# An attention and mixer kernel: tiled products gathered into fewer places of TensorE's order, seeds copied ahead of scalings, the fourth tile one stage later

## The chip, the cores and the metric

The kernel runs on one core of a Trainium2 chip. A core has a matmul engine (TensorE, PE in the profile; its weight loads are the row PEld), a vector engine (VectorE, DVE), a scalar engine (ScalarE, ACT), a general one (GpSimd, POOL) and a sync engine whose queue issues most DMAs (SyncE, SP). They run side by side and wait for each other through semaphores. The metric is the device time of one execution in microseconds (us); less is better.

## The reference

Two blocks, one after the other, all in float32. Linear attention without softmax (8 batches, 8 heads, 576 rows, head size 64), each head's output divided by its root mean square, and then a mixer on (8, 576, 512):

```python
kv = einsum('bhsd,bhse->bhde', k, v)
o = einsum('bhsd,bhde->bhse', q, kv)
x = o / sqrt(mean(o * o, axis=-1) + 1e-6) * g_norm      # heads side by side: (8, 576, 512)
h = maximum(x^T @ w_tok1, 0) @ w_tok2                   # over the 576 rows: 576 -> 256 -> 576
u = x + h^T
out = u + maximum(u @ w_ch1, 0) @ w_ch2                 # over the 512 columns: 512 -> 1536 -> 512
```

## The kernel before, in words

The first pass makes u; the second multiplies u with the channel weights by a two-level scheme of seven products for eight, and takes three quarters of the time. The change is in the first pass alone.

The first pass goes through the batches in four pairs. A pair has nine row tiles of 128 rows x 512 columns: four of each batch (rows 0 to 511) and one of the remaining 64 rows of both. They are made two at a time: attention "tiles" c = 0 to 3 (`attend`, L404, two row tiles each) and the remainder c = 4 (`attend_rem`, L418). Work of three pairs is interleaved by hand: `start` (L1241), `middle` (L1247) and the two lists `steady` (L1253) and then `last` (L1302) are strings of step names that `play` (L1192) issues one after the other; each engine executes its own instructions in that order. While a list does attention of pair p + 1 it does token mixing of pair p. Names of steps, with c or the row tile i as digits:

- `kv00 kv01 kv10 kv11` (L364): k^T v of batch 0 or 1 of the pair, half of the heads each, in 128x64 parts of the array; `e..` (L379) copies the result out on ScalarE; `l..` and `lq`, `lr` (L138, L149, L154) issue the loads of the next k, v, q, remainder of q.
- `a0` to `a4`: q times kv, in 64x64 parts of the array, into two PSUM banks, one for each row half; 64 matmul records each in the profile (`ps_o`), 32 for a4 (`ps_r`).
- `q` (squares, ScalarE, L446), `g` (times g_norm out of PSUM, VectorE, L435), `t` (sums of squares, VectorE, L460), then for a group of tiles `m` (mean, L468), `r` (root, ScalarE, L473), `i` (inverse with one correcting step, VectorE, L477), and the scaling of one row tile by the inverse: `s` on ScalarE as eight instructions (L493), `d` on VectorE (L500), `p` on GpSimd (L504).
- `h00 h01 h10 h11` (L532): w_tok1 products of a batch, accumulated over its four row tiles (`ps_h`); `hr` (L539): the remainder rows, 64 rows of the array, and then four relus on ScalarE (L127).
- `u0` to `u8` (L556): w_tok2 products of a row tile (`ps_u`), 4 records each, u8 in 128x64 parts. For i = 2, 4, 6 `z` (`seed`, L550) copies x into the bank beforehand on ScalarE, and the sum is copied out on ScalarE (L130); for the others VectorE adds x (L124). GpSimd issues the stores.
- `f`, digits, `x`, `b`: `f` loads a block of channel weights on SyncE's queue; a digit takes so many steps of their rounding (ScalarE scales, L163 and L166, VectorE clamps, shifts, adds, L169 to L178); `x` transposes row tiles on VectorE and `b` stores them.
- A name with a minus is a step of the pair whose attention began in the list before.

PSUM has eight banks in three pools (L96): "o" 2 (attention), "kv" 2 (k^T v), "h" 4 (token mixing). A tile that takes a bank waits until those that read its former contents are done. The k and v buffers are four, the raw weight buffers four.

Of the kernel before, what the change touches and what calls it, by code (L numbers as in the profile page):

```python
# [11 lines left out]
F32 = mybir.dt.float32  # L12
# [8 lines left out]
def kernel(  # L21
# [33 lines left out]
    P = 128  # L55
    B, S, DM = k.shape
    D = g_norm.shape[0]
# [7 lines left out]
    HP = H // 2  # L65
# [12 lines left out]
    def pool(name, bufs, side="left", stack=ctx, **kw):  # L78
        return stack.enter_context(tc.tile_pool(name=name, bufs=bufs, side=side,
                                                reuse_waits="tile", **kw))  # L80
# [15 lines left out]
    ps = {n: pool(f"ps_{n}", b, "left", psums, space=bass.MemoryType.PSUM)  # L96
          for n, b in (("o", 2), ("kv", 2), ("h", 4))}
# [34 lines left out]
    def matmul(*a, **kw):  # L132
        keep(nc.tensor.matmul(*a, **kw))  # L133
# [220 lines left out]
    def attention(pair, groups):  # L354
# [47 lines left out]
                           rhs=kvp[side][:, hp], start=True, stop=True)  # L402

        def attend(c):  # L404
            o = [ps["o"].tile([P, 2, HP, D], F32, name="ps_o", tag="o") for _ in range(2)]
            side = c // 2
            for t in range(2):
                for hp in range(HP):
                    for n in range(2):
                        for h in range(2):  # L410
                            r = ds(h * D, D)
                            matmul(o[h][ds(n * HF, HF), t, hp],
                                   lhsT=qT[2 * pair + side][r, hp, ds((2 * (c % 2) + t) * P + n * HF, HF)],
                                   rhs=kvp[side][r, hp, :D], start=True, stop=True)
            for h in range(2):
                bank[c, h] = o[h].rearrange("p t k d -> p (t k) d")

        def attend_rem():  # L418
            o = [ps["o"].tile([P, HP, D], F32, name="ps_r", tag="o") for _ in range(2)]
            for hp in range(HP):  # L420
                for side in range(2):
                    for h in range(2):
                        r = ds(h * D, D)
                        matmul(o[h][ds(side * HF, HF), hp], lhsT=q_rest[2 * pair + side][r, hp],
                               rhs=kvp[side][r, hp, :D], start=True, stop=True)
            for h in range(2):
                bank[4, h] = o[h]
# [86 lines left out]
        for c in range(5):  # L514
            if whole:
                steps |= {f"a{c}{t}": do(attend_tile, c, t) if c < 4 else attend_tile_rem
                          for t in range(parts(c))}
            else:
                steps[f"a{c}"] = do(attend, c) if c < 4 else attend_rem
            for h in range(parts(c)):  # L520
                steps |= {f"{n}{c}{h}": do(f, c, h) for n, f in zip("gqt", (gain, square, total))}
            for t in range(1 if c == 4 else 2):
                steps |= {f"{n}{c}{t}": do(f, c, t) for n, f in zip("spd", (scale, scale_pool, scale_vector))}
# [668 lines left out]
    def play(lines, after={}, **stages):  # L1192

        for name in " ".join(lines).split():
            if name.isdigit():
                for _ in range(int(name)):
                    next(stages["rounding"], lambda: None)()
            elif name[0] == "-":  # L1200
                stages["before"][name[1:]]()
            else:
                next(stages[s][name] for s in ("attention", "mixing", "more")
                     if name in stages.get(s, ()))()
# [28 lines left out]
    for block in tok1[2:] + tok2:  # L1233
# [11 lines left out]
        "a21 q21 g20 g21 t20 t21 m2", "h002 h012 r2 i2 d20", "a30 q30 g30", "a31 q31 s21 g31 t30", "h003 h013 t31 m3",  # L1245
        "a40 q40 r3 i3 d30 s31 g40 t40 m4 r4 w21 i4 s40 lq0 l10 l11 lr0 lr1"]
    middle = [  # L1247
        "kv00 e00 w31 w22 w23 w24", "h10 -lq1 w32 w33 w34", "kv01 e01 w41 w42",
        "h11 w43 w44", "hr l00", "a0 q00 g01 q01 g00 t00 t01", "u0 z2 f0", "u1 l01",
        "a1 q10 g11 q11 g10 t10 t11 m0 r0 lq0", "u2 i0", "kv10 e10 z4 d00", "u3 s01", "kv11 e11",  # L1250
        "u4 z6 f1", "a2 q20 g21 q21 g20 s10", "u5 t20 t21 f2", "a4 q40 g41 q41 g40 lr0 lr1 1", "u6 t40 t41 1 l10",
        "a3 q30 g31 q31 g30 lq1 d11", "u7 t30 t31 m2 r2 1 i2 p20 p21 s30", "u8 1 l11 d31"]
    steady = [[  # L1253
        "kv00 kv01 e00 e01 1 -d40 f3", "h00 1 x00", "h01 1 f4 b00", "a0 q00 g01 q01 g00 l00 1",
        "h10 t00 t01 1 x01", "h11 l01 1 x10 b01", "hr 1 x11 z2 f5 f6", "a1 q10 g11 q11 g10 lq0", "kv10 kv11 e10 e11 t10 t11 m0 r0",
        "u0 i0 1", "u1 1 d00 l10", "u2 s01 z4 1 f7", "a2 q20 g21 q21 g20", "u3 s10 t20 t21",
        "u4 z6 l11", "a4 q40 g41 q41 g40 lr0 lr1 1", "u5 d11 t40 t41 1", "a3 q30 g31 q31 g30 lq1",
        "u6 t30 t31 m2 r2 i2 d20 p21 s30", "u7 1 d31 1", "u8 1 b10 b11"], [
        "kv00 kv01 e00 e01 1 -d40 f8", "h00 1 x20", "h01 1 f9", "a0 q00 g01 q01 g00",
        "h10 t00 t01 1 x21", "h11 1", "hr 1 z2 f10", "a1 q10 g11 q11 g10", "kv10 kv11 e10 e11 t10 t11 m0 r0",  # L1260
        "u0 i0 1", "u1 1 d00 f11", "u2 s01 z4 1", "a2 q20 g21 q21 g20", "u3 s10 t20 t21",
        "u4 z6 1 f12", "a4 q40 g41 q41 g40", "u5 d11 t40 t41 1", "a3 q30 g31 q31 g30",
        "u6 t30 t31 m2 r2 i2 d20 p21 s30", "u7 1 d31 b20 b21", "u8 f13"]]

    attentions = [attention(0, ((0,), (1,), (2,), (3,), (4,)))]
    attentions += [attention(p, ((0, 1), (2, 3, 4))) for p in range(1, B // 2)]

    mixings = [token_mixing(p, (2, 4, 6)) for p in range(B // 2 - 1)]
    mixings.append(token_mixing(B // 2 - 1, range(2, 9), (0, 1)))
# [15 lines left out]
    play(middle, attention=attentions[1], mixing=mixings[0], before=attentions[0],  # L1285
         more=more, rounding=rounding)
    for n in range(1, B // 2 - 1):
        play(steady[n - 1], attention=attentions[n + 1], mixing=mixings[n], before=attentions[n],
             more=more, rounding=rounding)


# [5 lines left out]
    for i in range(2):  # L1297
# [2 lines left out]
    woven = fill[0][:4] + fill[1] + fill[0][4:]  # L1300

    last = [  # L1302
        "h00 2 -d40 2 o0", "h01 2 o1", "h10 2 o3", "h11 2 o2", "hr z2 1 o4", "u0 z3 1 c0", "u1 z4 1 c1 o5", "u2 z5 c2",
        "u3 z6 1 c3 o6", "u4 z7 1", "u5 z8 1", "u6 1 s0", "u7 s1 s2", "u8 s3 s4"]
    parts1 = [f for o in ORDER1 for f in split(1, o)]
    more = {f"c{i}": f for i, f in enumerate(t_sums(lambda n: uT[0][:, SB[n]]))}
# [97 lines left out]
```

## Time and profile before

| | us |
|---|---|
| three runs, median (lowest, highest) | 788.10 (786.69, 788.41) |
| the profiled execution | 787.48 |
| span of its core's instructions | 785.7 |
| first pass, first k-v product to the last product of u | 6.2 to 192.3 |
| `middle` (kv00 to the next kv00) | 37.2 to 74.3 |
| first `steady` list | 74.3 to 117.1 |
| second `steady` list | 117.1 to 160.7 |
| `last` | 160.7 to 192.3 |

| stretch | PE busy | DVE busy | ACT busy | POOL busy | DMA GB/s |
|---|---|---|---|---|---|
| 31 to 74 | 42.34 | 31.05 | 28.64 | 2.38 | 347 |
| 74 to 117 | 42.88 | 36.12 | 25.38 | 7.35 | 358 |
| 117 to 160 | 42.29 | 32.71 | 26.46 | 6.19 | 299 |
| 160 to 192 | 32.00 | 27.73 | 17.50 | 6.71 | 279 |

Each stretch of the second table but the last is 43 us long. Busy time of an engine is the union of its instructions; matmuls are pipelined and their ends are modelled, so starts of matmuls are the surer reading. The granted clock of TensorE is full throughout. In a row of a timeline the first number is the start, the second the length of a merged group, both in us from the span's start; "x64" is a number of records, and a bracket names idle time before the group and what ended it.

### The profile page before, as it was taken

To read this page: it belongs to the slowest core of one execution; us is meant where nothing else is said; L and a number is where in the kernel's file an instruction comes from. 1 tells how busy PE (TensorE), PEld (TensorE's weight loads), DVE (VectorE), ACT (ScalarE), POOL (GpSimd) and SP (SyncE) were. 2 spreads that over 40 slices of the span, in tenths; PEclk is the share of its full clock that TensorE was granted. 3 is DMA by queue.
4 is the path that set the end of the run, shared out by engine and by line. 5 is a ranking of instruction groups with operands and counts; after the bars stand their busy time and mean duration, and the time that the engine had idled before them with its cause. 6 is when DMAs were issued, how large, how long until landed. Compare 5 with 4: busy or idle time off the path is not lost.

```text
span 785.7 us, 14826 instructions
## 1 busy us (share of the span) xinstructions
PE 773.3 (98%) x5816; PEld 651.6 (83%) x5816; DVE 614.8 (78%) x909; ACT 269.5 (34%) x531; POOL 71.3 (9%) x84
## 2 busy tenths in 40 slices
PE   6999999999999999999999999999999999999998
PEld 6655545545888888999988899998889999889998
DVE  2877887795776868988778889776998885787977
ACT  2567463845110233521134242123352113325211
POOL 1001112123410000010100001010000101000111
PEclk9999999999999999999999999999999999999999
DMA  9999999787699795598897579889559989655864
GB/s 294 318 330 374 362 360 325 268 267 285 239 286 343 268 329 161 162 294 215 234 248 225 147 216 277 247 200 291 150 154 280 221 213 236 196 150 157 197 171 91
DMA packets 132613, 192.12 MB, mean 245 GB/s; under 512 B 13632, under 2 KB 92224, under 8 KB 132544
## 3 DMA queue, kind: packets, MB, share of 16 engines
q1 hardware_dynamic: 115984, 167.54, 67.8%
q0 software_dynamic: 14656, 22.02, 13.8%
q10 hardware_dynamic: 1904, 1.61, 0.7%
q8 instruction: 46, 0.75, 0.4%
q14 instruction: 23, 0.19, 0.1%
HBM read 138.31 MB, written 52.82 MB: 243 GB/s over the span
## 4 chain that ended last, share of the span: by engine, by line
PE 92%; ACT 3%; DVE 2%; DMA 2%; issue 0%; SPq 0%; ACTq 0%; DVEq 0%
PE ps_d L133 28%; PE ps_b L133 19%; PE ps_a L133 19%; PE ps_u L133 7%; PE ps_h L133 6%; PE ps_v L133 5%; PE ps_c L133 3%; PE ps_w L133 2%; PE ps_o L133 2%; PE ps_kv L133 2%; DMA raw<-in_moe_w_tok_dram 1%; ACT x L498 1%; DMA raw<-in_moe_w_ch_dram 1%; DVE ms L465 1%; DVE x L444 1%; ACT sq L448 1%
## 5 line engine op out<-in xcount | busy, mean ns | idle before, releaser
L133 PE MATMUL ps_d<-ui,w 128*128 128x256 f32 x504 | 118.7, 379 | 0.0
L130 ACT COPY ps_d<-ps_a 128x768 f32<-128x768 f32 (+1 forms) x56 | 32.0, 571 | 215.3 <-PE ps_a L133 215.3
L133 PEld LDWEIGHTS ps_d<-ui,w 128*128 128x128 f32 x504 | 95.1, 190 | 12.8 <-DVE v L124 0.2
L124 DVE TENSOR_TENSOR v<-v,v 128x1536 f32<-128x1536 f32 (+2 forms) x70 | 103.5, 1483 | 0.3
L133 PE MATMUL ps_b<-w,sv 128*128 128x128 f32 x672 | 84.6, 276 | 0.0
L133 PE MATMUL ps_a<-w,v 128*128 128x128 f32 x672 | 84.2, 275 | 0.0
L133 PEld LDWEIGHTS ps_a<-w,v 128*128 128x128 f32 x672 | 79.8, 192 | 0.2
L133 PEld LDWEIGHTS ps_b<-w,sv 128*128 128x128 f32 x672 | 79.5, 192 | 0.2
L133 PE MATMUL ps_u<-h,w_tok 128*128 128x512 f32 (+1 forms) x160 | 67.2, 606 | 0.8 <-ACT ps_u L130 0.7
L133 PE MATMUL ps_h<-x,w_tok 128*128 128x512 f32 (+1 forms) x160 | 65.6, 604 | 0.6 <-DVE x L502 0.4
L133 PE MATMUL ps_d<-w,v 128*128 128x128 f32 x528 | 66.2, 275 | 0.0
L133 PEld LDWEIGHTS ps_d<-w,v 128*128 128x128 f32 x528 | 62.7, 192 | 0.3
L127 ACT ACTIVATE v<-v 128x768 f32<-128x768 f32 (+1 forms) x54 | 42.6, 822 | 55.1 <-DVE v L124 55.1
L133 PE MATMUL ps_d<-w,sv 128*128 128x128 f32 x480 | 60.1, 275 | 0.0
L133 PEld LDWEIGHTS ps_d<-w,sv 128*128 128x128 f32 x480 | 57.1, 192 | 0.2
L133 PEld LDWEIGHTS ps_h<-x,w_tok 128*128 128x128 f32 (+1 forms) x160 | 26.0, 189 | 32.8 <-issue 27.6
L133 PEld LDWEIGHTS ps_u<-h,w_tok 128*128 128x128 f32 (+1 forms) x160 | 24.8, 179 | 31.5 <-issue 25.9
L1121 POOL DMA_DIRECT2D out_dram<-us x11 | 14.2, 1292 | 381.2 <-ACT us L130 268.9
L133 PE MATMUL ps_a<-uT,w 128*128 128x256 f32 x192 | 46.7, 379 | 0.0
L133 PE MATMUL ps_b<-ui,w 128*128 128x256 f32 x168 | 40.8, 379 | 0.0
L133 PEld LDWEIGHTS ps_a<-uT,w 128*128 128x128 f32 x192 | 36.3, 190 | 4.8
L444 DVE TENSOR_TENSOR x<-ps_o,g_sb 128x512 f32<-128x512 f32 x32 | 21.4, 687 | 23.7 <-PE ps_o L133 15.6
(145 smaller groups left out, 1213.0 us busy)
## 6 DMA issues: line engine op xcount, KB each, us to landing
w<-parts SPq DMA_DIRECT2D x168, 384.0 KB, 4.0
w<-parts SPq DMA_DIRECT2D x56, 192.0 KB, 3.0
uT<-blocks SPq DMA_DIRECT2D x36, 256.0 KB, 5.7
k_in<-in_k_dram SPq DMA_DIRECT2D x16, 512.0 KB, 9.0
qT<-in_q_dram SPq DMA_DIRECT2D x8, 1024.0 KB, 9.5
out_dram<-x POOLq DMA_DIRECT2D x16, 512.0 KB, 6.5
v_in<-in_v_dram SPq DMA_DIRECT2D x14, 512.0 KB, 9.1
raw<-in_moe_w_ch_dram SPq DMA_DIRECT2D x8, 768.0 KB, 10.5
```

Of the source, the lines that this page charges most:

```text
L124: keep(engine.tensor_tensor(out=o, in0=a, in1=b, op=op))
L127: keep(nc.scalar.activation(o, a, AF.Relu))
L130: keep(nc.scalar.copy(o, a))
L133: keep(nc.tensor.matmul(*a, **kw))
L444: keep(nc.vector.tensor_mul(x, bank[c, h], g_sb.to_broadcast([P, number(c), D])))
L448: keep(nc.scalar.activation(sq[c, h], bank[c, h], AF.Square))
L465: keep(nc.vector.tensor_reduce(stats_of(c)[0][:, h], sq[c, h], axis=AX.X, op=ALU.add))
L498: keep(nc.scalar.activation(x[:, k, h], x[:, k, h], AF.Copy, scale=inv[:, k, h]))
L1121: keep(nc.gpsimd.dma_start(to.rearrange("t p e -> p t e"), a, accum_op=ALU.add))
```

## The change

- In `middle` and both `steady` lists the places of the tiled products move: h11 follows h10 directly in `middle`; u0, u1 and u2 follow each other; kv10 and kv11 stand directly behind a1 in `middle` too; a4 stands directly behind a2; a3, with everything that belongs to it (q, g, t, s30, d31 and the load lq1), goes to the beginning of the next list, behind kv00, kv01 and the former pair's u8. In the second `steady` list a3 of the last pair stands between u7 and u8, and its scalings at the beginning of `last`.
- a0 and a4 take their banks from the pool "kv" in place of "o".
- In the `steady` lists the seeds z4 and z6 are issued ahead of the eight scalings s01 and s10.
- Tiles are grouped for their statistics as (0, 1), (2, 4), (3) in place of (0, 1), (2, 3, 4).
- The rounding steps, weight loads, transposes and block stores are placed anew along the lists; SyncE's queue gets the loads in another order (lq1, 1 MB, behind f3 and f8; l01 ahead of f0; f7 behind l11). In `last` one rounding step more is left to do.

```diff
         def attend(c):
-            o = [ps["o"].tile([P, 2, HP, D], F32, name="ps_o", tag="o") for _ in range(2)]
+            n = "o" if c else "kv"
+            o = [ps[n].tile([P, 2, HP, D], F32, name="ps_o", tag=n) for _ in range(2)]
...
         def attend_rem():
-            o = [ps["o"].tile([P, HP, D], F32, name="ps_r", tag="o") for _ in range(2)]
+            o = [ps["kv"].tile([P, HP, D], F32, name="ps_r", tag="kv") for _ in range(2)]
...
     middle = [
-        "kv00 e00 w31 w22 w23 w24", "h10 -lq1 w32 w33 w34", "kv01 e01 w41 w42",
-        "h11 w43 w44", "hr l00", "a0 q00 g01 q01 g00 t00 t01", "u0 z2 f0", "u1 l01",
-        "a1 q10 g11 q11 g10 t10 t11 m0 r0 lq0", "u2 i0", "kv10 e10 z4 d00", "u3 s01", "kv11 e11",
-        "u4 z6 f1", "a2 q20 g21 q21 g20 s10", "u5 t20 t21 f2", "a4 q40 g41 q41 g40 lr0 lr1 1", "u6 t40 t41 1 l10",
-        "a3 q30 g31 q31 g30 lq1 d11", "u7 t30 t31 m2 r2 1 i2 p20 p21 s30", "u8 1 l11 d31"]
+        "kv00 e00 w31 w22 w23 w24", "h10 -lq1 w32 w33 w34", "h11 w41 w42 w43 w44", "kv01 e01", "hr l00 z2",
+        "a0 q00 g01 q01 g00 t00 t01", "u0 l01 f0", "u1 z4", "u2", "a1 q10 g11 q11 g10",
+        "kv10 kv11 e10 e11 t10 t11 m0 r0 lq0", "u3 z6 i0 d00 s01 d11 f1", "u4 l10", "a2 q20 g21 q21 g20",
+        "a4 q40 t20 g41 q41 t21 g40 lr0 lr1", "u5 s10 t40 t41 m2 r2 f2 1", "u6 1 i2 p20 p21 l11 x00", "u7 1 1"]
     steady = [[
-        "kv00 kv01 e00 e01 1 -d40 f3", "h00 1 x00", "h01 1 f4 b00", "a0 q00 g01 q01 g00 l00 1",
-        "h10 t00 t01 1 x01", "h11 l01 1 x10 b01", "hr 1 x11 z2 f5 f6", "a1 q10 g11 q11 g10 lq0", "kv10 kv11 e10 e11 t10 t11 m0 r0",
-        "u0 i0 1", "u1 1 d00 l10", "u2 s01 z4 1 f7", "a2 q20 g21 q21 g20", "u3 s10 t20 t21",
-        "u4 z6 l11", "a4 q40 g41 q41 g40 lr0 lr1 1", "u5 d11 t40 t41 1", "a3 q30 g31 q31 g30 lq1",
-        "u6 t30 t31 m2 r2 i2 d20 p21 s30", "u7 1 d31 1", "u8 1 b10 b11"], [
...
+        "kv00 kv01 e00 e01 -d40 f3", "-u8 -a3 -q30 -g31 -q31 -g30 -t30 -t31 -m3 -r3 -lq1",
+        "h00 -i3 -d31 -s30 l00 b00 1 1", "h01 f4 x01 1", "a0 q00 g01 q01 g00", "h10 t00 t01 l01 b01 x10 1",
+        "h11 1 x11 1", "hr z2 f5 f6", "a1 q10 g11 q11 g10 lq0", "kv10 kv11 e10 e11 t10 t11 m0 r0", "u0 i0 1",
+        "u1 z4 d00 s01 l10", "u2", "a2 q20 g21 q21 g20", "a4 q40 t20 g41 q41 t21 g40 lr0 lr1", "u3 z6 d11 1",
+        "u4 s10 t40 t41 m2 r2 1 l11 f7", "u5 i2 d20 p21 1 1", "u6 1", "u7 1 1 b10 b11"], [
+        "kv00 kv01 e00 e01 -d40 f8", "-u8 -a3 -q30 -g31 -q31 -g30 -t30 -t31 -m3 -r3 -lq1",
+        "h00 -i3 -d31 -s30 x20 1", "h01 f9 x21 1", "a0 q00 g01 q01 g00", "h10 t00 t01 1 1", "h11 1 1", "hr z2 f10",
+        "a1 q10 g11 q11 g10", "kv10 kv11 e10 e11 t10 t11 m0 r0", "u0 i0 1", "u1 z4 d00 s01 f11", "u2",
+        "a2 q20 g21 q21 g20", "a4 q40 t20 g41 q41 t21 g40", "u3 z6 d11 1", "u4 s10 t40 t41 m2 r2 1",
+        "u5 i2 d20 p21 1", "u6 1 f12 b20 b21", "u7 1", "a3 q30 g31 q31 g30", "u8 t30 t31 m3 r3 f13"]]
...
-    attentions += [attention(p, ((0, 1), (2, 3, 4))) for p in range(1, B // 2)]
+    attentions += [attention(p, ((0, 1), (2, 4), (3,))) for p in range(1, B // 2)]
...
     last = [
-        "h00 2 -d40 2 o0", "h01 2 o1", "h10 2 o3", "h11 2 o2", "hr z2 1 o4", "u0 z3 1 c0", "u1 z4 1 c1 o5", "u2 z5 c2",
+        "h00 -i3 -d31 -s30 2 -d40 2 o0", "h01 2 o1", "h10 2 o3", "h11 2 o2", "hr z2 1 o4", "u0 z3 1 c0", "u1 z4 1 c1 o5", "u2 z5 c2",
```

## The prediction

> **What bounds the kernel now.** I read the page's busy shares and its chain of waits first, then TensorE's timeline over the first pass, then ScalarE's over the same stretch, then the waits after it.
>
> ```profile
> PE 773.3 (98%) x5816; PEld 651.6 (83%) x5816; DVE 614.8 (78%) x909; ACT 269.5 (34%) x531; POOL 71.3 (9%) x84
> ...
> PE 92%; ACT 3%; DVE 2%; DMA 2%; issue 0%; SPq 0%; ACTq 0%; DVEq 0%
> ```
>
> TensorE is busy 98% and the chain that ends last is TensorE's for 92%. From 160.68 us to the end its timeline names no wait at all: whatever TensorE does sooner in the first pass, the rest can start sooner. So the question is how much of TensorE's time in the first pass is not product. Each row: start, length, what; a bracket is an idle time and who ended it.
>
> ```profile
> 49.50 1.16 PE L133 MATMUL ps_o<-kvp,qT 64*64 64x64 f32 x64
> 50.59 3.70 PE L133 MATMUL ps_u<-h,w_tok 128*128 128x512 f32 x8
> ...
> 57.23 1.39 PE L133 MATMUL ps_kv<-v_in,k_in 128*64 128x64 f32 x40
> 58.54 1.98 PE L133 MATMUL ps_u<-h,w_tok 128*128 128x512 f32 x4
> ...
> 66.69 0.69 PE L133 MATMUL ps_r<-kvp,qR 64*64 64x64 f32 x32
> 67.31 1.98 PE L133 MATMUL ps_u<-h,w_tok 128*128 128x512 f32 x4
> 69.54 1.16 PE L133 MATMUL ps_o<-kvp,qT 64*64 64x64 f32 x64 [0.24 <-ACT sq L448]
> ...
> 94.97 2.55 PE L133 MATMUL ps_kv<-v_in,k_in 128*64 128x64 f32 x80
> 97.45 5.42 PE L133 MATMUL ps_u<-h,w_tok 128*128 128x512 f32 x12
> 102.80 1.16 PE L133 MATMUL ps_o<-kvp,qT 64*64 64x64 f32 x64
> 103.89 4.08 PE L133 MATMUL ps_u<-h,w_tok 128*128 128x512 f32 x8
> 107.91 0.69 PE L133 MATMUL ps_r<-kvp,qR 64*64 64x64 f32 x32
> 108.53 1.98 PE L133 MATMUL ps_u<-h,w_tok 128*128 128x512 f32 x4
> 110.45 1.33 PE L133 MATMUL ps_o<-kvp,qT 64*64 64x64 f32 x64
> 111.71 5.57 PE L133 MATMUL ps_u<-h,w_tok 128*128 128x512 f32 x16
> ...
> 146.69 1.98 PE L133 MATMUL ps_u<-h,w_tok 128*128 128x512 f32 x4
> 149.33 1.98 PE L133 MATMUL ps_u<-h,w_tok 128*128 128x512 f32 x4 [0.66 <-ACT ps_u L130]
> ```
>
> Read differences of starts, since lengths overlap by the pipeline. A full-array stretch of 12 records lasts 97.45 to 102.80 = 5.35, one of 4 lasts 108.53 to 110.45 = 1.92: eight records are 3.43, one is 0.429, and each stretch carries 5.35 - 12 x 0.429 = 0.20 us that is no product. An attention tile of 64 records takes 50.59 - 49.50 = 1.09, the remainder tile of 32 takes 67.31 - 66.69 = 0.62: 32 records are 0.47, so 0.155 is fixed. The k-v product: 40 records 1.31, 80 records 2.48, so 0.14 to 0.15 fixed. Every change of tiling is thus paid at the edges of the stretches on both sides: a tile put alone into a full-array stretch costs 0.155 and cuts it in two, 0.20 more.
>
> The second loss is waits. By the same differences: 67.31 to 69.54 is 2.23 where 4 records take 1.92 (0.31 wait); 103.89 to 107.91 is 4.02 where 8 take 3.63 (0.39); 110.45 to 111.71 is 1.26 for a tile of 1.09 (0.17). In the second `steady` list: 146.69 to 151.25, 8 records, 4.56 (0.93), then 151.87 to 153.90, 4 records (0.11), and the tile 153.90 to 155.18 (0.19). Sum 2.10.
>
> **The change part by part.** The matmuls are the same; only stretches and waits differ, so I count stretches by the play lists.
>
> *Fewer stretches.* In the second pair's list (`middle`) the full-array stretches before are h10, h11, u0-u1, u2, u3, u4, u5, u6, u7: nine; after, h10-h11, u0-u2, u3-u4, u5-u7: four. In each `steady` list u0-u2, u3-u4, u5, u6-u7 become u0-u2 and u3-u7: two fewer each. Nine fewer at 0.20 = 1.80. Attention stretches: a4 now follows a2 in the same tiling, in all three lists: three fewer at 0.155 = 0.47. kv10 and kv11 join in `middle`: 0.15. Moving a3 beside u8 saves nothing of its own (the tilings differ). Sum 2.41 us.
>
> [...]
>
> *Waits taken away.* The 0.31, 0.17, 0.11 and 0.19 stand at the start of a3 or inside it: a3 waits for the two "o" banks that a4 took just before (ScalarE's squares and VectorE's gains must have read them). With a4 and a0 in the "kv" banks and a3 a stage later, a3 finds banks that a2 left over ten matmuls ago. The 0.39 and 0.93 are u4 waiting for its seed:
>
> ```profile
> 146.79 2.01 ACT L498 ACTIVATE x<-x,inv 128x64 f32<-128x64 f32 x8
> 148.71 0.57 ACT L130 COPY ps_u<-x 128x512 f32<-128x512 f32 x1
> ```
>
> The seed copy z4 stood behind s01's eight scalings, though it needs none of them. After the change z4 is issued at u1, before s01: 2.0 us sooner against waits of 0.4 and 0.9, and u4 comes 0.5 later after u2, since a4 now stands between them. Sum 2.10, provided nothing takes their place.
>
> *New or moved waits, each against its cover.* (1) kv10 now needs a0's banks. a0 ends some 10 us earlier in a steady stage (h10, h11, hr, a1), 6.5 us in `middle` (u0-u2, a1); the squares and gains take 0.6 each, 2.6 in all: hidden. (2) a4 needs kv10's and kv11's banks, copied out by e10, e11 (0.25 each) 5.3 us before (u0-u2, a2): hidden. In `middle` kv00 of the next stage needs a4's gains; these follow a2's on VectorE and ScalarE, five gains and squares of 0.35 to 0.7, about 4 us after a4 against u5-u7, 5.35: hidden by about 1. (3) The copy out of u2 on ScalarE now stands behind s01, where it stood ahead. By the built program u3 takes u0's bank and only u5 takes u2's; u5 starts 5 us after u2 ends: hidden. (4) Each fourth tile gets statistics of its own: one mean (0.18), one root (0.23), four small VectorE operations (0.9) a stage, 1.3 us three times, against VectorE's 36 busy of 43 us in the first `steady` list: hidden but VectorE is fuller.
>
> (5) The fourth tile's scalings s30, d31 must now be done by h10 of the next stage, two matmuls in. From a3's end there are h00-h01 7.06, a0 1.09 and 1.8 of h10: 10.0 us; in the last stage u8 1.87, h00-h01 6.9 and 1.7: 10.5. In the trace a3 ended at 111.71 and s30 at 120.03, 8.3 us; in the second `steady` list 155.18 and 162.78, 7.6. Cover remains 1.7 to 2.9 us.
>
> ```profile
> 136.68 1.17 ACT L163 ACTIVATE w_ch<-raw 128x1024 f32<-128x1024 f32 x1 [7.44 <-DMA raw<-in_moe_w_ch_dram]
> ```
>
> (6) DMAs. The load queue is full until about 140 us (358 GB/s in 74 to 117). Moving a3 moves lq1, the 1 MB q load, with it: it waits on SyncE's queue for a3 in the next stage, and the loads of k and v, the block stores and f4 stand behind it. They have 8 transfers in flight before them, and a2 needs that q 25 us later: hidden. In the second `steady` list it moves behind f8, whose landing ends the row above: f8 lands 1.05 MB / 358 = 2.9 us sooner. TensorE is by then 1.6 (`middle`: 1.3 edges, 0.31 wait) + 1.1 (steady: 0.55 + 0.56) = 2.7 sooner. So ScalarE's relus stay late against hr as they are: they were done for u0 at 139.9, u0 started at 140.25. Cover 0.35 + 0.2 = 0.55 us; each us that f8 lands later than this costs one. No row shows this crossing; ends 0 and 2 us (the shifted 1 MB gives nothing back). I take 0.3 for (5) and (6) together, being nearest to the row that just fits.
>
> Downstream, the v products at 192.33 need sums that VectorE ended by 184.5, and one rounding step moves into the last stage (1.2 us): at 188 they still have 2 us or more.
>
> **Sum.** 2.41 + 2.10 - 0.3 = 4.2 us. The profiled execution took 787.48 (span 785.7), so 783.3 there; the median of the runs is 788.1, 0.6 higher, so 783.9.
>
> **The rivals.**
> A, the above: 783.9, chance 0.62. For: the edges cost the same to 0.01 us wherever they stand.
> B, only part arrives: f8 or the fourth tile holds TensorE 1 to 3 us in all: 785 to 786.7, say 785.7. For: the thin covers in (5) and (6), and ScalarE's two waits for raw loads, 4.2 and 7.4. Chance 0.20.
> C, the front moves and the end doesn't: VectorE's chain in the last stage is not sooner, since it starts from i3, and the v products wait for it; 787.5 to 788. Against: 2 us of cover and no wait there. Chance 0.10.
> D, slower. The fourth tile comes late in all three stages: ScalarE's root and scalings of it stand behind a rounding scale (L163) that waits for a raw load. It decides when the 8 us chain grows past 10; each us beyond costs three, in h10 of three stages. From 12.0 on the loss, 6, outweighs the 4.5 gained by over 0.2%. A wait as long as the 4.22 that ScalarE's timeline shows at 90.67 makes it 11.8 to 12.5, say 12.3: 2.3 x 3 = 7 us, less 4.5: 790.6. Against: by the order the scale in that place is f1, f6, f10, loads issued 10 us or more before. Chance 0.08.
>
> **How the numbers follow.** This kernel's measurement can tell about 0.2%, 1.6 us, from no change. Faster by more (below 786.5): A, and nine tenths of B, 0.80; within: the rest of B and C, 0.12; slower, D, 0.08. The range runs from the full gain without any new wait on the profiled run's level, 783.0 less 0.2, up to 786.5, the end of B; D and most of C are outside.
>
> **What would show it.** In TensorE's timeline: u3 to u7 as one x20 stretch and a2 with the remainder as neighbours in 1.56 us; no bracket at a3 or u4; v products at 187.9 to 188.2 instead of 192.32. Wrong steps: a bracket at u0 of the second `steady` list (f8), at h10 (fourth tile), at kv00 after `middle` (a4's gains). It would be wrong altogether if edges did not vanish with the stretches, or if the v products started at 192 after an idle time.

## The result, and the profile after

| | before | after |
|---|---|---|
| runs beside each other, five each, median (lowest, highest), us | 787.02 (786.52, 788.41) | 783.43 (783.29, 785.14) |
| the profiled execution, us | 787.48 | 783.41 |
| span of its core's instructions, us | 785.7 | 781.6 |
| first v product (end of the first pass), us | 192.32 | 188.20 |

The time is 0.9954 of the time before, 95% interval 0.9941 to 0.9968: faster by 3.6 us. The prediction was 783.9, and 783.3 for the profiled execution, which took 783.41. The whole gain is there when the second pass begins (4.12 us), and the second pass neither adds to it nor takes from it. Ratios leave out runs that are over 1.5% longer than the fastest of their kernel; below these are three of eight runs of the kernel with 104 more instructions, the traced one among them.

The page of the kernel after, TensorE's busy time and the chain that ended last, which is now TensorE's for 96% instead of 92%:

```profile
PE 769.3 (98%) x5816; PEld 650.6 (83%) x5816; DVE 617.4 (79%) x924; ACT 271.1 (35%) x534; POOL 70.5 (9%) x84
...
PE 96%; DVE 1%; DMA 1%; ACT 1%; SPq 0%; issue 0%; ACTq 0%
```

TensorE's timeline of the kernel after (start, length, what; no row between 37 and 188 has a bracket):

```profile
62.95 1.16 PE L133 MATMUL ps_o<-kvp,qT 64*64 64x64 f32 x64
63.93 1.01 PE L133 MATMUL ps_r<-kvp,qR 64*64 64x64 f32 x32
64.87 5.42 PE L133 MATMUL ps_u<-h,w_tok 128*128 128x512 f32 x12
...
101.57 1.16 PE L133 MATMUL ps_o<-kvp,qT 64*64 64x64 f32 x64
102.55 0.65 PE L133 MATMUL ps_r<-kvp,qR 64*64 64x64 f32 x32
103.13 8.85 PE L133 MATMUL ps_u<-h,w_tok 128*128 128x512 f32 x20
111.91 2.55 PE L133 MATMUL ps_kv<-v_in,k_in 128*64 128x64 f32 x80
...
137.91 5.42 PE L133 MATMUL ps_u<-h,w_tok 128*128 128x512 f32 x12
...
188.20 1.99 PE L133 MATMUL ps_v<-uT,w_ch 128*128 128x256 f32 x8
```

By starts, as in the prediction: u3 to u7 lasts 103.13 to 111.91, 8.78, which is 20 records at 0.429 and 0.20 for the one stretch. a2 and the remainder tile a4 together last 101.57 to 103.13, 1.56, one fixed 0.155 for both. In `middle` the same pair lasts 62.95 to 64.87, 1.92: 0.36 more. That is the only new loss after 38 us.

ScalarE's timeline of the kernel after, the load of f8 and the seed z4 of the second `steady` list:

```profile
132.35 1.13 ACT L163 ACTIVATE w_ch<-raw 128x1024 f32<-128x1024 f32 x1 [3.10 <-DMA raw<-in_moe_w_ch_dram]
...
139.74 0.58 ACT L130 COPY ps_u<-x 128x512 f32<-128x512 f32 x1
141.81 2.02 ACT L499 ACTIVATE x<-x,inv 128x64 f32<-128x64 f32 x8 [1.49 <-issue]
```

f8 lands 4.3 us sooner than before (132.35 for 136.68), where 2.9 had been estimated; the seed stands ahead of the eight scalings. A single landing says little about the 2.9, though: in the runs below whose edits leave f8, lq1 and the warm-up in place this scale starts anywhere from 132.38 to 133.90.

### The profile page after: what moved, and what is told of

Same layout as the page of the kernel before. It is cut to its first block, busy times and chain, and to the rows that moved or that the text cites. A ratio compares the mean times of both kernels' runs of the same rounds, so it can differ in the third digit from the quotient of the medians.

```text
span 781.6 us, 14842 instructions
## 1 busy us (share of the span) xinstructions
PE 769.3 (98%) x5816; PEld 650.6 (83%) x5816; DVE 617.4 (79%) x924; ACT 271.1 (35%) x534; POOL 70.5 (9%) x84
## 4 chain that ended last, share of the span: by engine, by line
PE 96%; DVE 1%; DMA 1%; ACT 1%; SPq 0%; issue 0%; ACTq 0%
PE ps_d L133 28%; PE ps_b L133 19%; PE ps_a L133 19%; PE ps_u L133 8%; PE ps_h L133 7%; PE ps_v L133 5%; PE ps_c L133 3%; PE ps_o L133 2%; PE ps_kv L133 2%; PE ps_w L133 2%; DMA raw<-in_moe_w_tok_dram 1%; DVE x L445 0%; PE ps_j L133 0%; DVE ms L466 0%; ACT x L499 0%; ACT sq L449 0%
## 5 line engine op out<-in xcount | busy, mean ns | idle before, releaser
L133 PE MATMUL ps_u<-h,w_tok 128*128 128x512 f32 (+1 forms) x160 | 64.7, 599 | 0.0
L133 PEld LDWEIGHTS ps_h<-x,w_tok 128*128 128x128 f32 (+1 forms) x160 | 26.2, 189 | 32.3 <-issue 27.8
L124 DVE TENSOR_TENSOR v<-ps_b,u 128x768 f32<-128x768 f32 x28 | 26.7, 954 | 15.3 <-PE ps_b L133 14.8
```

Source lines behind the costliest of these rows:

```text
L124: keep(engine.tensor_tensor(out=o, in0=a, in1=b, op=op))
```

## The experiments

All stand beside runs of the kernel before on the same chip. "v products" is their first start in TensorE's timeline.

| kernel | median, us | ratio to before (95%) | span | v products |
|---|---|---|---|---|
| after | 783.43 | 0.9954 (0.9941, 0.9968) | 781.6 | 188.20 |
| after, a2 and a4 apart | 784.61 | 0.9967 (0.9956, 0.9979) | 782.6 | 188.97 |
| after, a0 and a4 in "o" | 792.1 | 1.0055 (1.0037, 1.0073) | 790.8 | 197.2 |
| after, z4 behind s01 | 783.84 | 0.9958 (0.9944, 0.9973) | 781.8 | 188.49 |
| before, z4 ahead of s01 | 787.07 | 0.9995 (0.9986, 1.0005) | 785.2 | 191.86 |
| after, a3 back in its own list | 784.57 | 0.9966 (0.9953, 0.9979) | 782.5 | 189.09 |
| after, f8 behind lq1 | 785.73, one run | | 784.0 | 190.69 |
| after, s30 later | 784.25, one run | | 782.4 | 188.89 |
| after, a0 behind a3, twice | 784.40 | 0.9962 (0.9949, 0.9976) | 781.9 | 188.44 |
| after, a0 behind a3, once | 783.82 | 0.9962 (0.9949, 0.9974) | 780.8 | 187.51 |
| before, banks and seeds of after | 785.74 | 0.9978 (0.9969, 0.9986) | 783.8 | 190.37 |
| after, 104 more instructions ahead | 793.94 | 1.0065 (1.0042, 1.0088) | 797.6 | 204.37 |
| after, 148 more instructions ahead | 804.45 | 1.0206 (1.0189, 1.0223) | 802.5 | 208.74 |

### Edges: a2 and a4 taken apart

```diff
-        "a2 q20 g21 q21 g20", "a4 q40 t20 g41 q41 t21 g40", "u3 z6 d11 1",
+        "a2 q20 g21 q21 g20", "u3 z6 d11 1", "a4 q40 t20 g41 q41 t21 g40",
```

Likewise in the other two lists (in `middle` u4 goes between).

> The changed kernel with one u product put between a2 and a4 in each of the three lists; all else as changed. Edge theory: each list gets one more full-array stretch (0.20) and one more attention stretch (0.155), 0.355 each, 1.07 us in all; the v products, which start at 188.20 in the changed kernel, start at 189.2 to 189.3, the time is 784.5. Rival (edges are free, the gain was waits alone): 188.2, unchanged.

TensorE's timeline of this kernel, first `steady` list:

```profile
101.63 1.16 PE L133 MATMUL ps_o<-kvp,qT 64*64 64x64 f32 x64
102.72 1.98 PE L133 MATMUL ps_u<-h,w_tok 128*128 128x512 f32 x4
104.63 0.69 PE L133 MATMUL ps_r<-kvp,qR 64*64 64x64 f32 x32
105.26 7.13 PE L133 MATMUL ps_u<-h,w_tok 128*128 128x512 f32 x16
112.32 2.55 PE L133 MATMUL ps_kv<-v_in,k_in 128*64 128x64 f32 x80
```

Measured between the same neighbours: from a2 to the next k-v product in the first `steady` list 10.69 (101.63 to 112.32) for 10.34, from a2 to a3 in the second 10.70 for 10.34: 0.35 and 0.36, which is 0.20 + 0.155. In `middle` the pair costs the same 0.35 more, but the 0.36 loss of a4 is gone there, so the v products move by 0.77 and not by 1.07. The price of an edge is the same, 0.35 to 0.36, in all three lists.

### The seed, in both kernels

In the kernel after (second list likewise):

```diff
-        "u1 z4 d00 s01 l10", "u2",
+        "u1 d00 s01 z4 l10", "u2",
```

> The changed kernel with the seed z4 back behind the scalings s01 in both steady lists. My prediction gave the seed order 1.3 us of the gain (0.39 + 0.93); by that account the time goes to 784.7. The changed kernel's timelines say otherwise: s01 ends at 102.1 and 143.8, so z4 would be done by 102.7 and 144.4, and u4 starts at about 105.0 and 146.7; by this account nothing is lost and the v products start at 188.2.

Nothing returned at u4. From the middle's end to the last list, TensorE's starts are those of the kernel after to 0.01 us (69.87 to 111.56 and 111.56 to 156.21; after, 70.22 to 111.91 and 111.91 to 156.56). What had made room is that s01 itself goes sooner in the new order, which the prediction listed only as a possible cost, in (3): s01 is issued at u1, and no longer behind a rounding step and the copy out of u2. Here s01 starts at 99.72 and 142.95, in the kernel before at 103.44 and 146.79, so z4 is done by 102.2 and 145.5, while u4 starts only at about 104.6 and 146.3.

In the kernel before (second list likewise):

```diff
-        "u2 s01 z4 1 f7",
+        "u2 z4 s01 1 f7",
```

> The kernel before with one edit: in both steady lists z4 is issued ahead of s01 instead of behind it. Seed theory: the waits of u4 (0.39 and 0.93) go and the rest stays: the v products start at 191.0 instead of 192.32, the time falls by 1.3 us. Rival: the copy was not what u4 waited for, or another wait takes the place (a3's banks, whose squares come later by 0.5 us behind the copy): a fall of 0.7 or less.

The waits of u4 (0.39 and 0.93) are gone, but TensorE's timeline of this kernel shows what was behind them:

```profile
108.35 1.98 PE L133 MATMUL ps_u<-h,w_tok 128*128 128x512 f32 x4
110.64 1.34 PE L133 MATMUL ps_o<-kvp,qT 64*64 64x64 f32 x64 [0.31 <-ACT sq L448]
```

a3 comes sooner and now waits 0.37 ahead of its start (2.29 for a stretch of 1.92) and 0.18 inside, where it had waited 0.17 in all; in the second list it is 0.56 for 0.30. The first `steady` list gains nothing (103.00 to 117.31, 14.31 as before), the second 0.66. (In `middle` a3's wait of 0.31 was gone as well in this execution, but a4 took 0.37 longer there: the pause of which more below.) So the prediction's 1.3 for seeds was not the seeds' alone: those waits and a3's waits for its banks are one chain.

### Both kinds of waits taken away, the order left alone

The edit above, and the pool "kv" for a0 and a4, in the kernel before; no matmul moves.

> The kernel before, with nothing taken from the change but the pool kv for a0 and a4 and the seed z4 ahead of s01 in both steady lists; the order of the matmuls is as before, so no edge is saved. If the 2.10 us of waits counted in the prediction are what these two edits remove, the v products come at 190.2 instead of 192.32, span 783.6, 785.4 us. Seeds alone gave 0.5 of 1.3, since a3 then waited for its banks. Rival (in the old order the kv pool makes k-v products wait for the squares and gains of a0 and a4): 191 or later, 786.2 us or more.

This kernel's TensorE timeline has one bracket left after 38 us:

```profile
139.52 5.42 PE L133 MATMUL ps_u<-h,w_tok 128*128 128x512 f32 x12 [0.26 <-ACT h L127]
...
190.37 1.99 PE L133 MATMUL ps_v<-uT,w_ch 128*128 128x256 f32 x8
```

The v products come 1.95 us sooner than before, though this u0 now waits, and the time is 1.9 us less (785.74; 787.66 for the kernel before in those runs). Start to start, that wait costs 0.33 (2.81 from 136.71 for 2.48), and h10 in `middle`, which the edits do not touch, lost 0.33 less than before. So the edits removed 2.1 of waits, the predicted sum. The wait at u0 is step (6) as the prediction feared it: f8 was not moved here, its scale ran at 136.28, and ScalarE's relus were late for a TensorE that came sooner.

### The banks in the kernel after

```diff
-            n = "o" if c else "kv"
+            n = "o"
...
-            o = [ps["kv"].tile([P, HP, D], F32, name="ps_r", tag="kv") for _ in range(2)]
+            o = [ps["o"].tile([P, HP, D], F32, name="ps_r", tag="o") for _ in range(2)]
```

> The changed kernel with a0 and a4 back in the o banks, so that a4, directly behind a2, needs the two banks that a2 has just filled. Bank theory: a4 starts when a2's squares and gains have read them; in the changed kernel those end about 1.6 us after a2's end in both steady lists and 2.6 us after it in middle, so 5 to 6 us are lost and the time is 788 to 790, slower than before the change. Rival (two banks are enough, edges alone matter): unchanged at 783.4.

TensorE's timeline of this kernel:

```profile
62.92 1.16 PE L133 MATMUL ps_o<-kvp,qT 64*64 64x64 f32 x64
66.65 1.37 PE L133 MATMUL ps_r<-kvp,qR 64*64 64x64 f32 x32 [2.56 <-ACT sq L449]
67.95 7.87 PE L133 MATMUL ps_u<-h,w_tok 128*128 128x512 f32 x12
...
107.10 1.16 PE L133 MATMUL ps_o<-kvp,qT 64*64 64x64 f32 x64
109.79 0.69 PE L133 MATMUL ps_r<-kvp,qR 64*64 64x64 f32 x32 [1.53 <-ACT sq L449]
```

From a2 to the end of the u products, each `steady` list takes 1.76 us more and `middle` 5.56; the sum, 9.1, is the move of the v products. But not all of it is waiting. a4 directly behind a2 waits for a2's squares: the 1.76 in each `steady` list, and 2.75 in `middle`, where the squares also stand behind the scalings s01 on ScalarE (a4 starts 3.73 after a2 instead of 0.98). That is 6.3. The other 2.8 stand where this execution shows TensorE's granted clock at half, in `middle`. The stretch from 66 to 73 us; behind the busy times of the five engines stand the clock as a share of full, the DMA share and GB/s:

```profile
66.00:73.00 7.00, 6.35 (x38) 3.37 (x39) 3.87 (x8) 3.26 (x12) 0.00 (x0) 0.51 1.06 383
```

The stretch begins inside the wait for the squares, which ends at 66.65, and its mean clock is 0.51. Its 38 records are the 32 of a4 and six of u5 and u6: from 67.95 to 73 that makes about 0.84 us for one of the six (an estimate) instead of 0.43. The stretch of twelve lasts 7.80 by starts where the kernel after has 5.35. Behind the waits of 1.53 in the `steady` lists the next twenty records last 8.78, as in the kernel after. The four runs had mean clocks of 0.995, 0.995, 0.998 and 1.000, and the one at 1.000 took 789.71 us: 6.3 more than the kernel after, and inside the 788 to 790 that was expected. So the new pool is what makes the join possible: without it the change is slower than the kernel before, by the waits alone.

### a3 left in its own list

```diff
-        "u4 s10 t40 t41 m2 r2 1 l11 f7", "u5 i2 d20 p21 1 1", "u6 1", "u7 1 1 b10 b11"], [
+        "u4 s10 t40 t41 m2 r2 1 l11 f7", "u5 i2 d20 p21 1 1", "a3 q30 g31 q31 g30 lq1", "u6 t30 t31 m3 r3 1", "u7 i3 d31 s30 1 1 b10 b11"], [
```

Likewise in the other lists; statistics and scalings of the fourth tile move with it.

> The changed kernel with a3 back in its own list, between u5 and u6 in all three lists, its statistics still a group of its own. Edge theory: one more full-array stretch in each list, 0.20 x 3 = 0.6 us; no bank wait, since a4 stays in the kv banks and a2's o banks were read long ago; the v products start at 188.8, the time is 784.0. Rival (moving a3 to the next stage was what took its bank waits away): 0.3 to 0.5 more per list, 789 to 790 for the v products.

From a2 to h00, each `steady` list is longer by 0.20 (101.74 to 117.57, 15.83 for 15.63; 13.50 for 13.30): a3 alone cuts one full-array stretch in two. In `middle` the expectation of no bank wait failed: by starts a3 comes 0.23 late there and loses 0.24 inside. The last u products lose 0.32, of which the cause was not looked for. The delay of a3 is worth its edge in each list, and in `middle` those waits.

### f8 behind lq1

```diff
-        "kv00 kv01 e00 e01 -d40 f8", "-u8 -a3 -q30 -g31 -q31 -g30 -t30 -t31 -m3 -r3 -lq1",
+        "kv00 kv01 e00 e01 -d40", "-u8 -a3 -q30 -g31 -q31 -g30 -t30 -t31 -m3 -r3 -lq1 f8",
```

> The changed kernel with the load f8 put behind the q load lq1 (1 MB) and behind a3 on SyncE's queue in the second steady list. In the changed kernel f8 ends ScalarE's wait at 132.35 and the relus start at 134.40, 0.06 after hr's end. Crossing theory: f8 lands some 2.9 us later, the relus start near 137.3, u0 (137.91 in the changed kernel) waits for two of them until 138.3 to 138.5: 0.4 to 0.6 us lost. Rival (the load queue has slack here): the landing moves by less than 2.5 us and nothing is lost.

ScalarE's timeline of this kernel, and then TensorE's:

```profile
136.61 1.17 ACT L163 ACTIVATE w_ch<-raw 128x1024 f32<-128x1024 f32 x1 [6.79 <-DMA raw<-in_moe_w_ch_dram]
```

```profile
139.84 5.42 PE L133 MATMUL ps_u<-h,w_tok 128*128 128x512 f32 x12 [1.32 <-ACT h L127]
...
167.62 7.33 PE L133 MATMUL ps_h<-x,w_tok 128*128 128x512 f32 x20 [0.29 <-ACT x L499]
```

f8 lands 4.3 us later than in the kernel after, more than the 2.9 of the q load by its size, and u0 comes 1.40 later after a1 (4.97 for 3.57; TensorE was itself 0.5 later in this execution). Part of the 4.3 is not the edit's: by SyncE's timeline the issues of the block stores, which stand ahead of these loads in both kernels, ended 1.5 later in this execution (127.84 for 126.37). That leaves 2.8 for the q load.

So step (6) had the right place, price and cover. u0 starts 3.23 after f8's scale here (139.84 and 136.61); for u0 at 137.91, as in the kernel after, the scale may start as late as 134.7. The prediction had put the limit at 134.3: f8 2.9 sooner than before, and 0.55 of cover. And the loss has a second part that the prediction had put down to another step: ScalarE and VectorE are late by as much in the rest of the list, so the scalings s30 of the fourth tile end too late for h10 of `last`, 0.57 more. The same shows without any edit to f8 in the run with z4 behind s01: there f8's scale ran at 133.90, 1.55 later than in the kernel after, s30 came 1.34 later, and h10 waited 0.37 by its bracket, 0.64 by its starts. In the run with a2 and a4 apart the scale ran 1.04 later and s30 1.16 later, without a wait. Steps (5) and (6) are one chain, and in the kernel after it has 1.1 us left at h10 (s30 ends at 164.03, h10 reads that row tile at 165.14).

### s30 later

```diff
-        "h00 -i3 -d31 -s30 l00 b00 1 1",
+        "h00 -i3 -d31 l00 b00 1 1 -s30",
```

Likewise in the second list, behind h10, and in `last`. In the second list this changes the computation: h10 reads the row tile before it is scaled, and only h11 reads the scaled one.

> The changed kernel with s30 put behind a rounding scale: in the second steady list behind the squares of a0 and the scale of h10's line (in the first list and the last one only behind one digit). Cover theory: in the second list s30 would end near 131.3 while h10's third product needs it at 127.2, so TensorE waits about 4 us there and nothing elsewhere: v products at 192.2, the time 787.4. Rival (TensorE has other work, or the scalings are not what h10 needs): 188.2.

The first list lost nothing, with s30 ending at 84.1, and in `last` s30 stayed where it was by ScalarE's timeline. Only the second list lost, 0.67 at h11. So this run does not test the 4 us; what it shows is that the first list has room.

### a0 joined to a3

```diff
-        "kv00 kv01 e00 e01 -d40 f3", "-u8 -a3 -q30 -g31 -q31 -g30 -t30 -t31 -m3 -r3 -lq1",
-        "h00 -i3 -d31 -s30 l00 b00 1 1", "h01 f4 x01 1", "a0 q00 g01 q01 g00",
+        "kv00 kv01 e00 e01 -d40 f3", "-u8 -a3 a0 -q30 -g31 -q31 -g30 -t30 -t31 -m3 -r3 -lq1",
+        "h00 -i3 -d31 -s30 l00 b00 1 1", "h01 q00 g01 f4 x01 1 q01 g00",
```

In both `steady` lists:

> The changed kernel taken one step further in both steady lists: a0 directly behind a3 at the beginning, its squares and gains after the fourth tile's scalings; the full-array products h00 to h11 become one stretch. Edge theory: one full-array and one attention stretch fewer in each list, 2 x 0.355 = 0.71 us; v products at 187.5, the time 782.7. Rival (a0 waits for e00 and e01, or for the kv banks, which are read only at 74.5 and 114.8): a wait takes it back; by the timeline a3 ends at 75.5 and 117.2, so the cover is 0.9 us.

The first list gains the 0.36 of its edges. The second loses 0.59, and TensorE's timeline names no engine for it:

```profile
115.75 2.08 PE L133 MATMUL ps_o<-kvp,qT 64*64 64x64 f32 x122
118.45 0.34 PE L133 MATMUL ps_o<-kvp,qT 64*64 64x64 f32 x6 [0.63 <-issue]
```

(In all, a3 and a0 together take 2.97 here and 2.02 in the first list.) In the chain of waits of the kernel after, the 0.36 in `middle` looks the same, a pause in the midst of a tile:

```profile
64.11 0.34 PE ps_r L133 x23
64.45 0.14 issue
64.59 0.35 PE ps_r L133 x9
```

By starts a4 has such a pause in `middle` in six of the traced executions, of 0.1 to 0.4 us (it lasts 0.84 in this one, 0.94 in the kernel after); with z4 behind s01 it lasts 0.58, as in the `steady` lists, without a pause. Joined tiles do not pause as such: the 2.02 of the first list is 128 records at 0.47 for 32, and 0.155. The author's next question was the place of the pauses in TensorE's instructions. Each fp32 product of the program is four instructions (two weight loads and two matmuls: a row tile of u is two products and 4 records, and the page counts 5816 records of each kind); semaphore instructions come to it. Counted so in the trace of the kernel after, the pause in `middle` stands behind the 1473rd. The DMA queues on the page of the kernel after have a row of the name "instruction":

```profile
q8 instruction: 46, 0.75, 0.4%
```

These are 46 transfers of 16 KB. In the kernel after one of them runs from 62.08 to 63.08, and TensorE goes on 1.51 us after its end, at 64.59. In the kernel before one ends at 62.82, the 1473rd instruction comes 4.16 us after that, at 66.98, and there is no pause. In the kernel with a0 joined to a3 one starts between 116 and 117, ahead of the pause that ends at 118.45; the DMAs moved 355 GB/s from 114 to 121. That TensorE waits there for instructions of its own is a guess of the author's, called the fetch theory in the expectations; no view names what TensorE waited for.

The join in the first list only:

> The changed kernel with a0 directly behind a3 in the first steady list only. Edge theory: one full-array stretch (0.20) and one attention stretch (0.155) fewer: 0.36 us. Fetch theory: the pause of 0.84 us that took the gain of the second list's join is not there, because in the second list nothing is joined. v products at 187.8, span 781.2, 783.0 us. Rival (a joined tile of 128 records always waits): 188.2 or later.

As expected: no pause in the second list, v products at 187.51 (0.36 by the edges, 0.28 because the pause in `middle` is smaller, 0.08). It is not told apart from the kernel after by its time, 0.9962 and 0.9954 with intervals that overlap; no version of these clearly beats it.

### The pause moved by code alone

```diff
-        for _ in range(n):
-            matmul(o[:, :P], lhsT=ident, rhs=ident, start=True, stop=True)
+        m = n + {10: 11, 14: 15}[n]
+        w = n * P // m
+        for _ in range(m):
+            matmul(o[:, :w], lhsT=ident, rhs=ident[:, :w], start=True, stop=True)
```

and with 15 and 22 in place of 11 and 15:

> The changed kernel with the same warm-up time made of more and narrower matmuls: the two groups of 10 and 14 products of 128 columns (results never read) become 21 of 60 and 29 of 56 columns. That adds 104 TensorE instructions ahead of all that matters and changes nothing else. [...] Rival (the pause belongs to the tile or to its banks): it stays at the same records of a4, v products at 188.2.

> As before, but with 148 more TensorE instructions in the warm-up (25 products of 51 columns and 36 of 49 in place of 10 and 14 of 128). [...] So a new pause of 1 to 4 us inside the k-v products of the second steady list, and 0 to 2.5 at a3 at its beginning, the 0.36 in the second pair gone: v products at 189 to 193, likeliest 190.5; 785.5 us. Rival (instructions are no bound): 188.2, 783.4 us, no pause at the k-v products.

(The 29 products have 61 columns by the edit, not 56.) Both ask whether the pause keeps its place when only the number of instructions ahead of it changes. As total times they say nothing of it, since the edit itself cost 16 and 20 us at the start in the traced executions (last section); the traced run of the first took 799.41, where its runs went from 787.31 to 799.51. So only stretches are compared, here of the first:

```profile
80.46 0.65 PE L133 MATMUL ps_r<-kvp,qR 64*64 64x64 f32 x32
81.04 5.42 PE L133 MATMUL ps_u<-h,w_tok 128*128 128x512 f32 x12
```

In both, a4 in `middle` lasts 0.58 (80.46 to 81.04, and 84.83 to 85.41) where the kernel after has 0.94, and from the next kv00 to the v products both take 117.98, as the kernel after does. So with the order of work unchanged, the pause goes when the count ahead of it changes. One rival is left, the loads: everything stands 16 to 20 us later against them, and no run separates the two. The new pauses expected of the second kernel did not come: its k-v products of the second `steady` list last 2.48 (155.97 to 158.45) and its a3 1.09 (136.65 to 137.74), as in the kernel after (2.48 and 1.09). So the fetch theory stays a guess: the runs show where the pause goes away, and not what makes it.

## Why the prediction was right

- *Edges, 2.41.* Right. x20 in 8.78, the pair in 1.56, and 0.35 or 0.36 for each pair taken apart, 0.20 for a3 alone.
- *Waits, 2.10.* Right as a sum: the two edits alone, without any move, gave 1.95 at the v products. The split was wrong. The seeds alone gave 0.5 in the span, since a3's bank wait took over 0.38 and 0.26 of it, and in the new order the place of z4 is worth nothing by itself, because s01 itself goes sooner there.
- *(1) to (4), banks and VectorE.* No bracket at kv00, kv10 or u5. Right.
- *(5) and (6), 0.3.* Their links were right, but in the traced execution neither step cost anything: f8 landed 4.3 us sooner, where 2.9 was estimated (2.8 to 4.3 in the runs that leave its place alone). In its place stands 0.36 that was not in the sum at all, the pause in `middle`. That the two nearly cancel, so that the forecast gain of 4.2 comes within 0.1 of the 4.12 measured, is luck.
- *Sum.* 2.41 + 2.10 is 4.51; 4.51 - 0.36 = 4.15, and 4.12 was measured at the v products; the rest of the kernel passed it on unchanged.
- *Rivals.* B's places, u0 and h10, are real: a load that is 4.3 us late cost 2.0 in them. C did not come: no wait at the v products. D's place did wait in two of the kernels tried, by 0.6 us each, but its root is the late load of f8 and not the length of the fourth tile's own chain; its 790.6 was not reached by any of them.

## What to carry to other kernels

Where one engine is the bound, price what lies between its products by differences of starts, one fixed cost for each stretch of one shape (here 0.20 and 0.155), and check whether buffers allow the join: here the pool saved the same order of work 6.3 us of waits, and 2.8 more in the traced run, where the granted clock was 0.51 from 66 to 73 us. Look at waits in a row on one chain together: here the next one took over part of what the first gave up (0.5 of the 1.3 arrived). Many tiny products in a row lost 0.36 and 0.95 us here that no engine's row shows: ask whether such a pause keeps its place when only the instruction count ahead of it changes.

## What had not been expected of the hardware

*A warm-up of narrow products did not warm up.* TensorE's timelines of the kernel after, and of the one with 104 more instructions:

```profile
8.36 3.93 PE L133 MATMUL ps_j<-ident 128*128 128x128 f32 x28
```

```profile
8.44 12.63 PE L133 MATMUL ps_j<-ident 128*128 128x61 f32 x58
...
23.33 9.22 PE L133 MATMUL ps_j<-ident 128*128 128x60 f32 x42
32.34 4.86 PE L133 MATMUL ps_o<-kvp,qT 128*128 128x128 f32 x24
```

With 128 columns, records follow each other at 0.213 us for the first few and at 0.111 from 9.57 on. With 60 or 61 columns they stay at 0.21 to 0.22 by starts (58 in 12.56, 42 in 9.01), though TensorE had no gap from 8.4 to 32.3 us, and the k-v product between them takes 2.40 for 40 records, 1.39 at that place in the kernel after. Behind them 24 records of 128 columns still take 4.86, and the next eight 1.16. The run with 148 more shows the same: 72 records of 49 columns in 15.53 and 50 of 51 in 10.71, then 16 of 128 columns in 3.21, where 16 take 1.95 in the kernel after. The clock of the stretches is 1.00 throughout in all three, so these views do not show the cause. The trace's first record of a clock stands at 9.53 in the kernel after and at 11.66 in the kernel before, beside the change of pace in each (records from 9.57 and 11.68 on follow at 0.11). What kept the pace low with narrow products is not shown: no run separates their columns from other causes.

*A granted clock of 0.51 beside a wait.* The traced run of the kernel with a0 and a4 in "o" shows it from 66 to 73 us, where its one wait of 2.56 us ends; behind its two waits of 1.53 the pace was that of the kernel after, and one of its four runs had a mean clock of 1.000. Whether the wait brought the clock down is not shown.

*Transfers named "instruction" beside the data.* 46 of 16 KB, 1.00 us for the one ahead of the pause in `middle`, and pauses of 0.36 and 0.95 us by starts in tiles of 64x64 products, for which the views name no engine.
